# The last 256 KB of w_down as sixteen transfers of 1 to 15 and 8 rows, and final casts that wait for the matmuls alone

## The chip, the cores and the metric

The kernel runs on one core of a Trainium2 chip. Five engines execute their own instruction streams: TensorE (matmuls), VectorE, ScalarE, GpSimd and SyncE (SP), which here only issues DMA transfers. Data moves from HBM into SBUF through the core's 16 DMA engines. Engines and transfers are ordered by semaphores: an instruction waits until a semaphore has a value, and adds to one when it is done. The metric is the time of one execution in microseconds of device time; 180.47 us is the median of three runs before the change (179.78 to 180.82).

## What is computed

The reference is two layers of attention and a gated feed-forward block, run twice with the same weights, for four decode tokens:

```python
x = x + attn(layernorm(x), k_cache, v_cache, wq, wo)   # 32 heads, 8 kv heads, last 2048 of 8192 positions
x = x + glu(layernorm(x), w_gate, w_up, w_down)        # h = sigmoid(x @ w_gate) * (x @ w_up);  h @ w_down
x = x + attn(layernorm(x), k_cache, v_cache, wq, wo)
x = x + glu(layernorm(x), w_gate, w_up, w_down)
```

x is 4 x 512 (bf16), the feed-forward width is 1792, so w_down is 1792 x 512, 1.8 MB. Almost all bytes are the K and V windows (16.8 MB each for the 4 sequences) and the weights, which are read again in the second round as far as they were not kept.

## The kernel before

The kernel is written as a plan. `P.op(engine, name, duration, emit, r, w, banks)` records an operation with what it reads and writes as tokens, and `_Plan.op` turns these into dependencies: a reader depends on the last writer of a token, a writer on the readers since then or, without readers, on the last writer (lines 57 to 69), and users of one PSUM bank from different engines depend on each other. `_schedule` then orders each engine's operations by an estimate of their times; SP's transfers keep the order in which they were recorded. `_assign_sync` gives every operation a semaphore: each compute engine has one of its own, and SP's transfers take 24 in turn, each transfer also depending on the one that used its semaphore before. It then keeps the waits that are not already implied.

SBUF holds an arena of 50 slots of 4 KB per partition. `load` (line 496) records a transfer into a pair of slots with `dma` (line 395), which is one `dma_start` on SP. Transfers are recorded as soon as slots come free, so SP's queue runs far ahead of their use: the second w_gate and w_up, then w_down, wait in the queue while attention is still being computed.

w_down is laid out so that partition p holds rows 14p to 14p+13; a piece (a, b) takes b-a of these 14 rows of each partition. In the second round `bounds_of(1)` makes three pieces: rows 0 to 7 (1 MB), 8 to 11 (512 KB), 12 and 13 (256 KB, one contiguous 2 KB row for each of 128 partitions). They are the last three transfers before the output.

At the very end `glu(1, ..., last=True)` computes the gate and up projections, transposes them on VectorE, forms h in `hT` (line 1348), and multiplies with w_down piece by piece (`e_d`, line 1356): for each of the 14 rows four matmuls, one for each 128 output columns, so 32, 16 and 8 matmuls for the three pieces, all adding into one PSUM bank in which the residual x already lies (line 1306). Each piece's matmuls wait for that piece's transfer. Then four casts (line 1373) move 128 columns each to `orow`, a view of `ebuf`: ScalarE takes groups 0 and 2, VectorE 1 and 3. Each names as written, besides its own token `("oc", g)`, the token `("e", g // 2)` of its half of `ebuf`; groups 0 and 1 so share one, and 2 and 3. Last, SP issues the output transfer, which waits for the casts.

Of the kernel before, what the change touches and what calls it, by code (L numbers as in the profile page):

```python
# [254 lines left out]
class _SlotPool:  # L255
# [16 lines left out]
    bw_8k=421.0, bw_4k=409.0, bw_3k=405.0, bw_1k=347.0,  # L272
# [6 lines left out]
def build(nc, A_x, A_k, A_v, A_wq, A_wo, B_wg, B_wu, B_wd, out, cfg=None):  # L279
# [11 lines left out]
    NB, SQ, D = A_x.shape  # L291
# [7 lines left out]
    NFC = F // 128  # L299
# [16 lines left out]
    wd_d = B_wd.rearrange("(p k) n -> p k n", p=128)  # L316
# [5 lines left out]
    with es:  # L322
        def sb(name, shape, dt):
            return es.enter_context(nc.sbuf_tensor(name, shape, dt))
# [35 lines left out]
        hT = sb("hT", [128, NFC * NB], BF16)  # L360
# [13 lines left out]
        PBS = (2, 3)  # L374
# [8 lines left out]
        def tile_ap(s):  # L383
            return arena[:, s * SLOT:(s + 2) * SLOT]

        def tok(s):
            return [("slot", s), ("slot", s + 1)]

        def c_dve(n, rate=None):
            return tm["dve_fix"] + n * (tm["dve_f32"] if rate is None else rate)  # L390
# [4 lines left out]
        def dma(name, dst, src, w, r=(), rate="bw_4k", nbytes=None, sem=None):  # L395
            if nbytes is None:
                nbytes = dst.partition_size() * dst.free_nbytes()
            o = P.op("sync", name, 0.0, lambda e, dst=dst, src=src: e.dma_start(dst, src),  # L398
                     r=r, w=w, dma_bytes=nbytes, dma_rate=tm[rate])
            if sem is not None:  # L400
                o.sem = sem
                o.inc = 16
            return o


        loads = []
        where = {}
        left = {}
# [51 lines left out]
        def need(name):  # L460
            while name not in where:
                take_load()
            return where[name]

        def done(name):
            left[name] -= 1
            if left[name] == 0:
                s = where.pop(name)
                if name in on_free:
                    on_free[name](s)  # L470
                else:
                    pool.release(s)
                fill()
# [13 lines left out]
        def load_half(name, src, rate, size, where_):  # L487
            left[name] = 1
            homes[name] = [where_]
            on_free[name] = lambda s: hfree.add(s)  # L490

            def emit(s):
                dma(str(name), slot_ap(s)[:, 0:size], src, w=[("slot", s)], rate=rate)
            loads.append((name, emit))

        def load(name, n_use, rate, part):
            left[name] = n_use

            def emit(s):
                src = part[1]  # L500
                dst = tile_ap(s)[:, 0:part[0]]
                if name[0] in ("wg", "wu"):
                    dst = tile_ap(s).rearrange("p (f n) -> p f n", f=2)[:, :, 0:F]
                elif len(src.shape) == 3 and not part[2]:
                    dst = dst.rearrange("p (f n) -> p f n", f=src.shape[1])
                dma(str(name), dst, src, w=tok(s), rate=rate)
            loads.append((name, emit))
# [8 lines left out]
        def bounds_of(k):  # L516

            return [(a, min(NFC, a + 4)) for a in range(0, NFC, 4)] if k < NG else bounds[:-1] + [(bounds[-1][0], NFC - 2), (NFC - 2, NFC)]
# [31 lines left out]
        def load_glu(k):  # L550
            for nm, src in (("wg", wg_d), ("wu", wu_d)):
                if k == 0:
                    for c in range(NC):
                        load_half((nm, c, k), src[:, c, :], "bw_3k", F,
                                  (((GB, 0), (GB, 1), (GA, 0), (Y, 0)), ((Y, 1), (Z, 0), (GB, 0), (GB, 1)))[nm == "wu"][c])
                    continue
                for cc in range(NC // 2):
                    load((nm, cc, k), 2, "bw_3k", (2 * F, src[:, 2 * cc:2 * cc + 2, :], False))
            for (a, b) in bounds_of(k):
                if k == 0:  # L560
                    load_half(("wd", a, k), wd_d[:, a:b, :].rearrange("p k n -> p (k n)"), "bw_4k", (b - a) * D,
                              ((GA, 0), (Y, 0), (Y, 1), (Z, 0))[a // 4])
                else:
                    load(("wd", a, k), 1, "bw_8k", ((b - a) * D, wd_d[:, a:b, :], False))


        STASH = SB + PBS
# [48 lines left out]
        def keep_half(s):  # L616
# [9 lines left out]
             r=[("ones_f",)], w=[("e", 0)])  # L626
# [6 lines left out]
        for jh in range(2):  # L633
            for bp in range(2):
                for i in range(2):
# [7 lines left out]
                         r=[("ones_f",), ("perm",)], w=[("perm", jh, bp, i)])  # L643
# [5 lines left out]
             r=[("ones_f",)], w=[("msk_s",)])  # L649
        P.op("vector", "msk_s2", 100.0, lambda v: v.tensor_scalar(msk_s[:, :], msk_s[:, :], -1.0e30, None, ALU.mult),  # L650
             r=[("msk_s",)], w=[("msk_s",)])
        P.op("gpsimd", "msk_m", 200.0,
             lambda g: g.affine_select(msk_m[:, :], ones_f[:, 0:2], [[-1, 2]], ALU.is_equal, 0.0, base=0, channel_multiplier=1),
             r=[("ones_f",)], w=[("msk_m",)])
        P.op("vector", "sel_f", 200.0,
             lambda v: v.tensor_reduce(sel_f[:, :], perm[:, :].rearrange("p (g x) -> p x g", x=NR), AXX, ALU.add),
             r=perms, w=[("sel_f",)])
        P.op("gpsimd", "sel_b", 200.0, lambda g: g.tensor_copy(sel_b[:, :], sel_f[:, :]),
             r=[("sel_f",)], w=[("sel_b",)])
        P.op("vector", "sel_r", 100.0,  # L660
             lambda v: v.tensor_reduce(sel_r[:, :], sel_f[:, :].rearrange("p (g y) -> p y g", g=2), AXX, ALU.add),
             r=[("sel_f",)], w=[("sel_r",)])
        P.op("vector", "eyew", 200.0,
             lambda v: v.tensor_reduce(eyew[:, 96:128], ident.rearrange("p (a j) -> p j a", a=4), AXX, ALU.max),
             r=[("e", 0), ("eyew0",)], w=[("eyew",)])
        P.op("vector", "maskp", 200.0,
             lambda v: v.tensor_reduce(maskp[:, :], ident.rearrange("p (a j) -> p a j", a=4), AXX, ALU.max),
             r=[("e", 0)], w=[("maskp",)])
        P.op("vector", "maskb", 100.0,
             lambda v: v.tensor_reduce(maskb[:, :], maskp[:, :].rearrange("p (j b) -> p b j", j=2), AXX, ALU.max),  # L670
             r=[("maskp",)], w=[("maskb",)])
# [3 lines left out]
             r=[("eyew",)], w=[("maske",)])  # L675
        P.op("vector", "mod4", 100.0,
             lambda v: v.tensor_reduce(mod4[:, :], ey.rearrange("p (e m) -> p m e", m=REP), AXX, ALU.max),
             r=[("eyew",)], w=[("mod4",)])
# [4 lines left out]
             r=[("mod4",), ("maskp",)], w=[("selm",)])  # L683
# [4 lines left out]
             r=[("e", 0)], w=[("permo",)])  # L688
# [4 lines left out]
             r=[("sel_r",)], w=[("maskr",)])  # L693

        o = P.op("scalar", "x_in", 1300.0, lambda e: e.dma_start(x_nat, x_d), w=[("prow",)])
# [585 lines left out]
        def glu(k, b0, b1, last=False):  # L1281
# [31 lines left out]
            for n, nm in enumerate(("wg", "wu")):  # L1313
                for c in range(NC):
                    name = (nm, c if k == 0 else c // 2, k)
                    s = need(name) + (0 if k == 0 else c % 2)

                    def e_g(pe, c=c, s=s, n=n):
                        last = None
                        for g in range(4):  # L1320
# [4 lines left out]
                         r=[("slot", s), ("xn",)], w=[("gu", n)], banks=(gub[n],))  # L1325
                    done(name)
                if n == 0:
                    variance()
                P.op("vector", "gt%s%d" % (nm, k), c_dve(NF),
                     lambda v, n=n: v.transpose(ebuf[:, 0:NF],  # L1330
                                                ps[:, gub[n], 0:NF].rearrange("p (x k) -> p k x", k=NFC)),
                     r=[("gu", n)], w=[("e", 0), ("e", 1)], banks=(gub[n],))

                if n == 0:
                    P.op("vector", "gs%d" % k, c_dve(NH),
                         lambda v: v.tensor_tensor(egv, tv, lnr[:, 0:nb].unsqueeze(1).broadcast_to([128, NFC, nb]), ALU.mult),
                         r=[("e", 0), ("e", 1), ("lnr", 0)], w=[("eg",), ("q", 0)])
                    P.op("scalar", "gex%d" % k, c_act(NH),
                         lambda a: a.activation(eg[:, 0:NH], eg[:, 0:NH], ACTF.Exp, scale=-1.0),
                         r=[("eg",)], w=[("eg",)])  # L1340
# [3 lines left out]
                         r=[("eg",), ("lnd",)], w=[("eg",)])  # L1344
# [4 lines left out]
                 r=[("e", 0), ("e", 1), ("eg",), ("q", 0)], w=[("hT",)])  # L1349
            if last:  # L1350
                x_rows()
                for (a, b) in bounds_of(k):
                    name = ("wd", a, k)
                    s = need(name)

                    def e_d(pe, a=a, b=b, s=s):
                        last_ = None
                        src = tile_ap(s)
                        for fc in range(a, b):
                            for g in range(NC):  # L1360
                                o = (fc - a) * D + g * 128
                                last_ = pe.matmul(ps[32 * g:32 * g + NB, PBS[0], 0:128], hT[:, fc * NB:(fc + 1) * NB],
                                                  src[:, o:o + 128], start=False, stop=(fc == NFC - 1),
                                                  skip_group_check=True)
                        return last_
                    P.op("tensor", "gd%d_%d" % (k, a), (b - a) * 200.0, e_d,
                         r=tok(s) + [("hT",)], w=[("orow",)], banks=(PBS[0],))
                    done(name)
                orow = ebuf[0:NB, 0:half].bitcast(BF16)
                for g in range(NC):  # L1370
                    eng, f = ("scalar", "copy") if g % 2 == 0 else ("vector", "tensor_copy")
                    P.op(eng, "oc%d" % g, c_dve(128),
                         lambda e, g=g, f=f: getattr(e, f)(orow[:, g * 128:(g + 1) * 128], ps[32 * g:32 * g + NB, PBS[0], 0:128]),
                         r=[("orow",)], w=[("oc", g), ("e", g // 2)], banks=() if g else (PBS[0],))
                dma("out", out_d, orow, w=[("out_dram",)], r=[("oc", g) for g in range(NC)], rate="bw_1k", nbytes=NB * D * 2,
                    sem=("out",))
                return
            for (a, b) in bounds_of(k):
                name = ("wd", a, k)
                s = need(name)  # L1380

                def e_d(pe, a=a, b=b, s=s):
                    last = None
                    src = slot_ap(s)
                    for fc in range(a, b):
# [7 lines left out]
                     r=tok(s)[:1] + [("hT",)], w=[("cb",)], banks=(CB,))  # L1393
# [6 lines left out]
                 r=[("cb",)] + xts, w=xts, banks=(CB,))  # L1400
# [16 lines left out]
        load_wo(HKV // 2 - 1)  # L1417
        loads.append((GB, lambda s: None))
        load_glu(0)
        load_wq(1)  # L1420
        v_tiles = {}
# [21 lines left out]
        attn_second()  # L1443
        attn_add(2)
        glu(1, 0, NB, True)
        assert not loads

# [67 lines left out]
```

## Time and profile before

One execution was profiled:

| | |
|---|---|
| time of the profiled execution | 179.53 us |
| its span, first to last instruction | 177.7 us |
| median of three runs | 180.47 us (179.78 to 180.82) |
| granted TensorE clock, mean | 0.923 (0.50 after 160 us) |
| bytes read from HBM | 70.26 MB, 395 GB/s over the span |
| last three w_down transfers issued (SP) | 152.91, 157.23 and 158.57 us |
| output issued / landed | 176.04 / 177.27 us |

The page gives each engine's busy time and its share of the span, then the span in 40 slices whose digits are busy tenths. The chain of waits follows the last instruction back through what released it. A timeline line has start, duration, engine, line, operation, what it writes and reads, and in brackets how long the engine was idle before and what ended that. PEld is TensorE loading the small operand of a matmul. SPq and the like are an engine's sequencer, which waits, branches and issues. A landing is the moment at which a DMA engine's share of a transfer adds to the transfer's semaphore; a transfer is complete when all have.

### The profile page before, as it was taken

What the parts mean: (1) busy time and instruction counts of PE and PEld (TensorE: products, weight loads), DVE (VectorE), ACT (ScalarE), POOL (GpSimd) and SP (SyncE); (2) the same over time, 40 slices, a digit from 0 to 9 for tenths busy, and PEclk for the clock granted to TensorE, in tenths of its full rate; (3) what the DMA queues carried; (4) which work ended last, traced back from release to release, by engine and by line L of the source; (5) the groups of instructions that cost most, each with busy time, mean ns of one, the idle gap of its engine ahead of it and who ended that gap; (6) DMA issues with size and microseconds to landing.
All of it is one profiled execution on the core that took longest, in us unless ns stands there. A gap on an engine that the chain in (4) does not pass through costs nothing.

```text
span 177.7 us, 3886 instructions
## 1 busy us (share of the span) xinstructions
PE 102.3 (58%) x1641; PEld 55.0 (31%) x1653; DVE 104.7 (59%) x256; ACT 32.7 (18%) x87; POOL 21.6 (12%) x88
## 2 busy tenths in 40 slices
PE   0635326472933626506427847455967999876663
PEld 0202111242521512403415842141323444345321
DVE  7308997848476384593573573332299999752351
ACT  2002031221030300301102001000143454440011
POOL 6100010101010100100101000000011443342000
PEclk9999999999999999999999999999988888885555
DMA  5999999999999999999999999999999999999990
GB/s 193 426 426 424 422 422 413 420 420 419 419 417 422 415 422 422 413 417 424 420 419 422 405 406 368 411 395 408 410 382 365 428 424 422 411 421 403 408 367 23
DMA packets 12738, 70.52 MB, mean 397 GB/s; under 512 B 1320, under 2 KB 1328, under 8 KB 6576
## 3 DMA queue, kind: packets, MB, share of 16 engines
q1 hardware_dynamic: 12712, 70.26, 97.1%
q8 instruction: 13, 0.21, 0.5%
q14 instruction: 5, 0.04, 0.1%
q10 hardware_dynamic: 8, 0.00, 0.0%
HBM read 70.26 MB, written 0.00 MB: 395 GB/s over the span
## 4 chain that ended last, share of the span: by engine, by line
DMA 35%; DVE 32%; PE 21%; SPq 3%; issue 3%; ACT 3%; POOL 0%; DVEq 0%; ACTq 0%
DMA arena<-in_A_v_cache_dram 15%; DMA arena<-in_B_w_down_dram 13%; DVE arena L841 11%; PE ps L870 7%; PE ps L960 5%; DVE nmax L883 5%; DMA arena<-in_A_wq_dram 4%; DMA arena<-in_B_w_gate_dram 4%; SPq L398 3%; PE ps L859 2%; DVE arena L1051 2%; DVE ebuf L918 2%; DVE nmax L887 2%; DVE mxt L891 2%; PE ps L1147 2%
## 5 line engine op out<-in xcount | busy, mean ns | idle before, releaser
L841 DVE STREAM_TRANSPOSE arena<-arena 128x1024 f32<-128x1024 f32 x32 | 37.0, 1203 | 0.0
L870 PE MATMUL ps<-arena,qbd 128*32 128x512 bf16 x256 | 25.6, 536 | 0.1
L883 DVE TENSOR_REDUCE nmax<-ps 128x1 f32<-128x512 f32 x16 | 10.9, 682 | 19.3 <-PE ps L870 19.2
L960 PE MATMUL ps<-ebuf,arena 128*128 128x8 bf16 x576 | 17.6, 168 | 7.3 <-DMA arena<-in_A_v_cache_dram 4.1
L859 PE MATMUL ps<-msk_m,msk_s 128*32 128x512 bf16 x64 | 8.4, 518 | 23.0 <-DVE arena L841 21.8
L960 PEld LDWEIGHTS ps<-ebuf,arena 128*128 128x128 bf16 x576 | 16.7, 104 | 9.2 <-DMA arena<-in_A_v_cache_dram 5.1
L898 ACT ACTIVATE prow<-ps,nmax 128x512 bf16<-128x512 f32 x16 | 11.0, 687 | 34.1 <-DVE nmax L895 29.5
L834 ACT CAST qbd<-ps 128x256 bf16<-128x256 f32 x16 | 5.9, 370 | 44.9 <-PE ps L870 35.0
L927 POOL CAST s<-psm 128x1 bf16<-128x1 f32 x9 | 1.7, 188 | 83.6 <-ACT prow L898 83.6
L870 PEld LDWEIGHTS ps<-arena,qbd 128*32 128x32 bf16 x256 | 8.4, 121 | 10.3 <-issue 7.2
L782 PE MATMUL ps<-arena,xn 128*4 128x512 bf16 x64 | 8.4, 579 | 5.4 <-DMA arena<-in_A_wq_dram 5.1
L913 ACT CAST prow<-ps 128x512 bf16<-128x512 f32 x16 | 9.4, 586 | 11.4 <-PE ps L1042 3.0
L1321 PE MATMUL ps<-arena,xn 128*4 128x448 bf16 x64 | 7.5, 552 | 3.1 <-DMA arena<-in_B_w_up_dram 1.9
L918 DVE STREAM_TRANSPOSE ebuf<-prow 128x256 f32<-128x256 f32 x16 | 7.0, 435 | 3.9 <-ACT prow L913 3.7
L859 PEld LDWEIGHTS ps<-msk_m,msk_s 128*32 128x32 bf16 x64 | 1.7, 98 | 24.1 <-DVE arena L841 22.6
L794 DVE STREAM_TRANSPOSE ebuf<-ps 128x512 f32<-128x512 f32 x3 | 2.1, 716 | 10.6 <-PE ps L782 10.5
L760 ACT ACTIVATE lnv<-ps 128x4 f32<-128x4 f32 x4 | 0.7, 174 | 41.4 <-PE ps L756 41.4
L1042 PE MATMUL ps<-arena,ebuf 128*32 128x512 bf16 x112 | 8.2, 417 | 0.1
L829 PE MATMUL ps<-qh,eyew 32*128 32x64 bf16 x64 | 5.6, 217 | 4.2 <-ACT qbd L834 2.4
L968 DVE TENSOR_TENSOR onb<-ps,rinv 128x16 bf16<-128x16 f32 x9 | 1.6, 183 | 9.5 <-PE ps L960 9.5
L1147 PE MATMUL ps<-onp,arena 128*128 128x16 bf16 x144 | 5.3, 175 | 2.4 <-DVE onp L983 2.1
L1330 DVE STREAM_TRANSPOSE ebuf<-ps 128x448 f32<-128x448 f32 x4 | 2.6, 650 | 5.8 <-PE ps L1321 5.8
(111 smaller groups left out, 132.7 us busy)
## 6 DMA issues: line engine op xcount, KB each, us to landing
arena<-in_A_v_cache_dram SPq DMA_DIRECT2D x27, 1024.0 KB, 22.4
arena<-in_A_k_cache_dram SPq DMA_DIRECT2D x16, 1024.0 KB, 25.1
arena<-in_A_wq_dram SPq DMA_DIRECT2D x4, 1024.0 KB, 7.8
arena<-in_A_wq_dram SPq DMA_DIRECT2D x8, 512.0 KB, 6.5
arena<-in_A_wo_dram SPq DMA_DIRECT2D x3, 1024.0 KB, 26.2
arena<-in_B_w_down_dram SPq DMA_DIRECT2D x4, 512.0 KB, 6.4
arena<-in_B_w_gate_dram SPq DMA_DIRECT2D x4, 448.0 KB, 8.6
arena<-in_B_w_up_dram SPq DMA_DIRECT2D x4, 448.0 KB, 5.0
```

Source lines behind the costliest of these rows:

```text
L782: last = pe.matmul(ps[32 * hh:32 * hh + NB, qb, :], xn[:, c * NB:(c + 1) * NB], src[:, o + hh * 512:o + (hh + 1) * 512], start=(c == 0), s ...
L841: P.op("vector", "T%d_%d" % (h, t), c_dve(1024), lambda v, v32=v32: v.transpose(v32, v32), r=[("slot", 4 * h + t)], w=[("slot", 4 * h + t)])
L859: last = pe.matmul(ps[32 * gi:32 * gi + 32, bank, :], msk_s[:, :], msk_m[:, :].unsqueeze(1).broadcast_to([128, 256, 2]), start=True, stop= ...
L870: last = pe.matmul(ps[32 * gi:32 * gi + 32, bank, :], qbd[:, q0:q0 + 32], kt[:, cp // 2, cp % 2, jh * NJ:(jh + 1) * NJ, :], start=False, s ...
L883: lambda v: v.tensor_reduce(nmax[:, k2:k2 + 1], ps[:, bank, :], AXX, ALU.max),
L898: lambda a: a.activation(prow[:, :].rearrange("p (m x t) -> p m x t", x=32, t=2), ps[:, bank, :].rearrange("p (m t x) -> p m x t", x=32, t ...
L913: P.op("scalar", "pc" + tag, c_act(512), lambda a: a.copy(prow[:, :], ps[:, pb, :]), r=[("ppb", pb)], w=[("prow",)], banks=(pb,))
L918: P.op("vector", "pt" + tag, c_dve(256), lambda v: v.transpose(et, prow[:, :].bitcast(F32)), r=[("prow",)], w=[("e", k2)])
L960: last = pe.matmul(ps[:, ob, bp * 8:bp * 8 + 8], src[:, j * 128:(j + 1) * 128], ev[:, j % 2, j % 16 // 2, x0:x0 + 8], start=(j == 0), stop ...
L1042: last = pe.matmul(ps[32 * g:32 * g + 32, ob, :], ew[:, g, mq, t], src.rearrange("p (m t d) -> p t m d", t=2, d=128)[:, t], start=(n == 0) ...
L1147: last = pe.matmul(ps[:, WB, c * NR:(c + 1) * NR], tile_ap(s)[:, o + r_ * D + c * 128:o + r_ * D + (c + 1) * 128], ov[:, r_ * NR:(r_ + 1) ...
L1321: last = pe.matmul(ps[32 * g:32 * g + NB, gub[n], 0:NF], xn[:, c * NB:(c + 1) * NB], slot_ap(s)[:, g * NF:(g + 1) * NF], start=(c == 0), s ...
```

## The change

The 256 KB piece is no longer one transfer of 128 partitions but sixteen, of 1, 2, 3 and so on to 15 partitions, and a last one of 8 (together 128). Each has its own semaphore and its own token `("part", i)`; the eight matmuls of the piece read all sixteen tokens. The parts take over the dependencies of the first one, which waits for the slots. Since semaphores are given in turn, six of the parts wait for the transfers that used theirs before. The other edit takes `("e", g // 2)` out of what the four final casts write, so that each depends on the matmuls alone.

```diff
+                elif b < NFC:
+                    load(("wd", a, k), 1, "bw_8k", ((b - a) * D, wd_d[:, a:b, :], False))
                 else:
-                    load(("wd", a, k), 1, "bw_8k", ((b - a) * D, wd_d[:, a:b, :], False))
+                    load_last(("wd", a, k), a, b)
+
+        PARTS = list(range(1, 16)) + [8]
+        def load_last(name, a, b):
+            left[name] = 1
+            def emit(s):
+                dst = tile_ap(s)[:, 0:(b - a) * D].rearrange("p (f n) -> p f n", f=b - a)
+                p0, first = 0, None
+                for i, n in enumerate(PARTS):
+                    o = dma("%s_%d" % (name, i), dst[p0:p0 + n], wd_d[p0:p0 + n, a:b, :],
+                            w=[("part", i)] + (tok(s) if i == 0 else []), rate="bw_4k")
+                    if first is not None:
+                        o.deps.update(first.deps)
+                    first = first or o
+                    p0 += n
+            loads.append((name, emit))
...
                     P.op("tensor", "gd%d_%d" % (k, a), (b - a) * 200.0, e_d,
-                         r=tok(s) + [("hT",)], w=[("orow",)], banks=(PBS[0],))
+                         r=tok(s) + [("hT",)] + ([("part", i) for i in range(len(PARTS))] if b == NFC else []),
+                         w=[("orow",)], banks=(PBS[0],))
...
-                         r=[("orow",)], w=[("oc", g), ("e", g // 2)], banks=() if g else (PBS[0],))
+                         r=[("orow",)], w=[("oc", g)], banks=() if g else (PBS[0],))
```

More of the change, by code (lines that the diff above doesn't have):

```diff
@@ L562, in load_glu @@
                               ((GA, 0), (Y, 0), (Y, 1), (Z, 0))[a // 4])
-                else:
-                    load(("wd", a, k), 1, "bw_8k", ((b - a) * D, wd_d[:, a:b, :], False))
+                elif b < NFC:
+                    load(("wd", a, k), 1, "bw_8k", ((b - a) * D, wd_d[:, a:b, :], False))
+                else:
+                    load_last(("wd", a, k), a, b)
[12 more added lines that the diff above has]
+                    p0 += n
+                assert p0 == 128
+            loads.append((name, emit))
         STASH = SB + PBS
```

## The prediction

> **What bounds the kernel now.** I read the page's share of busy time and its slices first, then the chain that ended last in order of time, then the timeline of the last microseconds, then those microseconds cut into windows.
>
> ```profile
> span 177.7 us, 3886 instructions
> PE 102.3 (58%) x1641; PEld 55.0 (31%) x1653; DVE 104.7 (59%) x256; ACT 32.7 (18%) x87; POOL 21.6 (12%) x88
> DMA  5999999999999999999999999999999999999990
> q1 hardware_dynamic: 12712, 70.26, 97.1%
> ```
>
> No engine is busy for more than 59%, while the transfers are above 90% in 38 of 40 slices: the kernel reads 70 MB without a pause, and nothing in this change alters that. What is left is the tail behind the last byte. The chain, start and length in us:
>
> ```profile
> 157.23 16.74 DMA arena<-in_B_w_down_dram
> 173.97 0.04 issue
> 174.01 0.60 PE ps L1362 x16
> 174.61 0.03 issue
> 174.64 0.41 PE ps L1362 x8
> 175.05 0.02 issue
> 175.07 0.27 ACT ebuf L1373
> 175.34 0.02 issue
> 175.36 0.28 DVE ebuf L1373
> ```
>
> The chain does not run through the transfer that is changed. Its DMA piece ends at 173.97, which is the landing of the 512 KB piece before it; 16 matmuls of that piece follow, and only then the 8 of the 256 KB piece. The timeline of the same stretch:
>
> ```profile
> 174.01 0.31 PEld L1362 LDWEIGHTS ps<-arena,hT 128*4 128x4 bf16 x16 [0.50 <-DMA arena<-in_B_w_down_dram]
> 174.64 0.10 PEld L1362 LDWEIGHTS ps<-arena,hT 128*4 128x4 bf16 x8 [0.32 <-DMA arena<-in_B_w_down_dram]
> 175.07 0.54 ACT L1373 CAST ebuf<-ps 4x128 bf16<-4x128 f32 x2 [5.00 <-PE ps L1362]
> 175.36 0.61 DVE L1373 CAST ebuf<-ps 4x128 bf16<-4x128 f32 x2 [3.20 <-ACT ebuf L1373]
> 176.04 0.34 SPq L398 DMA_DIRECT2D out_dram<-ebuf  x1
> ```
>
> VectorE sits idle until ScalarE's first cast is over, though both read the same finished sums. The windows show how the DMA engines run out one after the other (columns: busy us of each engine, clock, DMA share, GB/s):
>
> ```profile
> 171.00:172.00 1.00, 0.63 (x12) 0.13 (x4) 0.70 (x2) 0.00 (x0) 0.00 (x0) 0.50 1.00 404
> 172.00:173.00 1.00, 0.22 (x12) 0.23 (x16) 0.16 (x1) 0.00 (x0) 0.00 (x0) 0.50 0.70 274
> 173.00:174.00 1.00, 0.80 (x32) 0.51 (x20) 0.00 (x0) 0.00 (x0) 0.00 (x0) 0.50 0.39 135
> ```
>
> The trace's semaphore records give the landings engine by engine. The 512 KB piece lands on the first of 16 engines at 171.94 and on the last at 173.97; the 256 KB piece between 172.61 and 174.60. So each engine needs 0.63 to 0.67 us for its eight 2 KB rows (packets start 80 ns apart), and the engines stand 2.0 us apart before they begin. The lags behind the first are 0.08, 0.26, 0.32, 0.45, 0.56, 0.59, 0.71, 0.92, 0.99, 1.29, 1.72, 1.73, 1.74, 1.80 and 2.03 us. Instruction fetches of 16 KB, 0.93 to 1.12 us each on one engine, are what I take to have made most of it.
>
> **The change part by part.** The profiled execution took 179.53 us with a span of 177.7. It lies 0.94 below the median of 180.47 and below all three runs shown; the sum is made on it and carried over as a difference.
>
> *Casts.* Before: ScalarE's first cast 175.07 to 175.33, VectorE's two 175.36 to 175.65 and 175.68 to 175.97, ScalarE's second done at 175.61. After the change VectorE waits for the matmuls only, so its first starts beside ScalarE's at 175.07 and its second ends at 175.07+0.28+0.02+0.29 = 175.67. The output's issue follows 0.07 later, as now. Gain 0.30. ScalarE's second cast already overlapped VectorE's first without stretching either (258 against 255 ns, 282 against 293), so the bounds are narrow, 0.27 to 0.30. Nothing else is queued behind these casts.
>
> *Waits of TensorE.* The last eight matmuls now wait for sixteen semaphores. In the built program that is eight instructions that only wait, then the ninth wait on the first weight load. The trace has no such row of waits; single ones last 51 ns on TensorE, and the next weight load starts 75 ns after such a wait starts (110.07 to 110.15, 39.89 to 39.96). Eight cost 0.41 to 0.60. They begin when the sequencer has sent off the 16 matmuls before them. It runs ahead: the instruction behind the last eight matmuls is recorded at 174.66, 0.02 after the first of them starts. So the waits begin between 174.03 and 174.19 and the last matmuls between 174.44 and 174.79, against 174.64 now. The array itself, taking four matmuls each 0.107, would be free at 174.40. I take 174.10+0.60 = 174.70, the only measured distance to a next instruction: a loss of 0.06, bounds -0.24 and +0.15. If no wait cost anything, the matmuls of the 512 KB piece would still hide the transfer until 174.40.
>
> *Sixteen issues on SP.* Before, the changed transfer is issued at 158.57 and takes 2.12 because the queue is full. An issue that does not block costs 0.33 to 0.61, the output's four rows 0.34; sixteen take 5.3 to 9.8 us. Six of them also wait for semaphores last used by six value loads, landed between 143.6 and 156.3, before the issue. A full queue held 80 to 107 descriptors an engine, and the fullest engine gets 32 for this transfer instead of 9; 23 more drain at 0.14 each in 3.2 us. All are out by 158.6+9.8+3.2 = 171.6 at worst, the earliest engine turns to them at about 171.5, and SP has nothing else before the output at 176.04. Cost 0; the cover is those 13 us of queued weights.
>
> *The landing of the 256 KB.* The input and the output, four rows each, show four data packets and four semaphore packets, while 128 rows make sixteen semaphore packets. So a part of n rows occupies n engines. If each part begins with the same engine, the loads are 16, 15, 14 down to 9, then 7 down to 0 rows, in place of 8 each. A row costs 0.080 and its part's semaphore 0.006. Bounds: with the many rows on the engines that are early, the last landing is 174.00; with them on the late ones, 173.97+16x0.086 = 175.34; shuffled at random, half the orders lie under 175.00 and one in fifteen under 174.66. Everything up to 174.66 is hidden behind the waits. No row names the engines, so this is the open term: 0 to +0.7. I take 0, since lags grow in an orderly ramp of 2.0 us and the new loads are a ramp of 1.3 us: they either fit together or oppose.
>
> [...]
>
> Sum: -0.30 +0.06 +0 +0 = -0.24: 179.29 in a profiled execution, 180.2 for the median.
>
> **Rivals.** *The ramp opposes the lags.* The last landing is 174.9 to 175.34, the matmuls start 0.04 to 0.1 later instead of at 174.64: +0.3 to +0.8, with the casts 0.0 to +0.5, so 180.5 to 181.0. For it: random orders mostly do this. Against: nothing but the ramp's shape.
>
> *Slower: the small transfers queue by number.* The kernel never had more than 11 transfers in flight; with the parts it would have 23. If the queue holds at most 12, the last five parts go out only after 174.0, when the 512 KB has landed, at 0.34 each; the output needs 1.23 from issue to landing, so the last part lands near 177.0, +2.4-0.3: 182.6. With 16 only the last part waits, for 173.97: 175.3, +0.65-0.3, about 180.8. It decides from a limit of 14 down. Against: issue blocked at 7, 8, 9 and 10 transfers, always near the same number of descriptors.
>
> *The transfer is hidden and the waits too.* The matmuls start at 174.40: -0.24-0.30, so 179.9. For it: the sequencer's lead; against: 75 ns a wait.
>
> **How the numbers follow.** Forecast 0.47 (own range 179.9 to 180.4, which includes the third rival), opposing ramp 0.35, limit by number 0.13, and 0.05 for other executions in which the engines stand further apart than in this profile and the ramp recovers up to 1 us. About 0.5%, 0.9 us, is what a measurement tells from no change. Faster by more needs 179.57, which the terms reach only with that last case or by the spread of the runs (179.78 to 180.82): 0.11. Slower by more needs 181.37: the limit by number, and the worst third of the opposing ramp with the port rule's bound: 0.24. Within: 0.65. The range 179.5 to 181.7 leaves out the stronger half of the limit by number.
>
> **What would show it.** VectorE's first cast starting with ScalarE's; eight waits on TensorE between the last two groups of matmuls and their spacing; sixteen issues on SP ended before 171; the last part's landing against 174.6. The prediction is wrong if the last matmuls wait for a landing after 174.7, or if an issue on SP begins after 172.

## The result and the profile after

The changed kernel took 182.01 us in the median of 15 runs, the kernel before 180.82 us beside it: 1.0077 times as long, with a 95% interval of 1.0055 to 1.0099. A second set of runs gave 1.0093 (1.0058 to 1.0127). So it is slower, by 1.4 us in the first set and 1.7 us in the second, where 180.2 us and no measurable change had been forecast.

The profiled execution after took 182.01 us with a span of 180.2 us. The page's first line and its transfers:

```profile
span 180.2 us, 3909 instructions
DMA  4999999999999999999999999999999999999960
q1 hardware_dynamic: 12824, 70.26, 96.1%
```

As before, the transfers are busy to the end and as many bytes move. The end of the chain, start and length in us:

```profile
158.42 18.01 DMA arena<-in_B_w_down_dram
176.42 0.04 issue
176.47 0.59 PE ps L1382 x8
177.06 0.37 issue
177.43 0.41 PE ps L1382 x8
177.84 0.02 issue
177.87 0.28 DVE ebuf L1394
178.15 0.32 DVEq L1495
```

Two things are new: the 0.37 us between the two groups of matmuls, and one cast in place of two. The timeline shows the casts side by side:

```profile
177.40 0.13 PEld L1382 LDWEIGHTS ps<-arena,hT 128*4 128x4 bf16 x8 [0.62 <-issue]
177.87 0.60 DVE L1394 CAST ebuf<-ps 4x128 bf16<-4x128 f32 x2 [3.97 <-PE ps L1382]
177.87 0.54 ACT L1394 CAST ebuf<-ps 4x128 bf16<-4x128 f32 x2 [7.77 <-PE ps L1382]
178.55 0.27 SPq L398 DMA_DIRECT2D out_dram<-ebuf  x1
```

The windows of the same stretch (columns: busy us of each engine, clock, DMA share, GB/s):

```profile
171.00:172.00 1.00, 0.00 (x0) 0.00 (x0) 0.00 (x0) 0.00 (x0) 0.00 (x0) 0.50 0.99 404
172.00:173.00 1.00, 0.98 (x16) 0.38 (x16) 0.01 (x1) 0.00 (x0) 0.00 (x0) 0.50 0.93 330
173.00:174.00 1.00, 0.37 (x8) 0.00 (x0) 0.86 (x2) 0.00 (x0) 0.00 (x0) 0.50 0.64 178
174.00:175.00 1.00, 0.06 (x6) 0.07 (x8) 0.00 (x0) 0.00 (x0) 0.00 (x0) 0.50 0.41 139
```

Compare bytes with busy share. Before, 274 GB/s went with a share of 0.70, which is 391 GB/s for a full share. Here 178 GB/s go with 0.64, which is 278. The engines are busy and move less. The trace's packet records say how: a packet of 8 KB takes 314 ns before, and 401 to 448 ns between 172.6 and 173.7 here; one of 4 KB 223 ns on average in the half microsecond from 173.0 against 159; one of 2 KB 117 against 84. The packets of 8 KB and 4 KB belong to transfers that the change does not touch.

The spans differ by 2.5 us, but not all of that is the change. I followed the last of 16 engines from piece to piece in the landings:

| | before | after | difference |
|---|---|---|---|
| last landing of w_up | 170.25 | 171.98 | +1.73 |
| from there to that of the 1 MB piece | 2.48 | 2.91 | +0.43 |
| to that of the 512 KB piece | 1.24 | 1.53 | +0.29 |
| to that of the 256 KB | 0.63 | 0.47 | -0.16 |
| to the last eight matmuls | 0.04 | 0.54 | +0.50 |
| casts | 0.97 | 0.68 | -0.29 |

The first packet of a part moves at 172.26, so the 1.73 us were there before any of them. Of the 1.73, 0.82 us is there already on the first of the 16 engines (168.15 before, 168.97 after), and 0.91 is a wider spread of the engines (2.10 and 3.01 us). Both differ between executions: in a second profile of the changed kernel, shown below, w_up lands at 170.97 with a spread of 2.07. The execution profiled before was an early one (179.53 against a median of 180.82 in these runs). The rest of the 2.5 us, +0.77, lies behind w_up.

### The profile page after: what moved, and what is told of

It is laid out like the page before. It is cut to its first block, busy times and chain, and to the rows that moved or that the text cites. A ratio compares the mean times of both kernels' runs of the same rounds, so it can differ in the third digit from the quotient of the medians.

```text
span 180.2 us, 3909 instructions
## 1 busy us (share of the span) xinstructions
PE 101.9 (57%) x1641; PEld 54.9 (30%) x1653; DVE 103.9 (58%) x256; ACT 32.7 (18%) x87; POOL 21.6 (12%) x88
## 4 chain that ended last, share of the span: by engine, by line
DVE 35%; DMA 33%; PE 20%; issue 4%; SPq 3%; ACT 3%; POOL 1%; DVEq 0%; ACTq 0%
DMA arena<-in_A_v_cache_dram 15%; DMA arena<-in_B_w_down_dram 14%; DVE arena L861 11%; PE ps L890 7%; DVE nmax L903 5%; DMA arena<-in_A_wq_dram 4%; SPq L398 3%; PE ps L980 3%; PE ps L879 2%; DVE nmax L907 2%; DVE arena L1071 2%; DVE mxt L911 2%; DVE ebuf L938 2%; PE ps L1167 2%; ACT prow L918 2%
## 5 line engine op out<-in xcount | busy, mean ns | idle before, releaser
L1062 PE MATMUL ps<-arena,ebuf 128*32 128x512 bf16 x112 | 7.6, 392 | 0.2 <-DVE nmax L915 0.2
```

The lines of the kernel that those rows point to most:

```text
L1062: last = pe.matmul(ps[32 * g:32 * g + 32, ob, :], ew[:, g, mq, t], src.rearrange("p (m t d) -> p t m d", t=2, d=128)[:, t], start=(n == 0) ...
```

## The experiments

### The terms by themselves

Casts alone, on the kernel before:

```diff
-                         r=[("orow",)], w=[("oc", g), ("e", g // 2)], banks=() if g else (PBS[0],))
+                         r=[("orow",)], w=[("oc", g)], banks=() if g else (PBS[0],))
```

> The kernel before with the edit to the four casts alone; the 256 KB of w_down stays one transfer of 128 rows. Every theory has the casts as a term of its own, -0.30 us (0.27 to 0.30): VectorE's and ScalarE's first casts start together right behind the last matmul, and the output is issued 0.30 earlier. If the change's loss were hidden in the casts (two engines reading one PSUM bank at once, say), this kernel would gain less than 0.2, and the stretch would be seen in the durations of the four casts.

Measured: 0.9974 of before (0.9943 to 1.0005).

```profile
175.83 0.10 PEld L1362 LDWEIGHTS ps<-arena,hT 128*4 128x4 bf16 x8 [0.33 <-DMA arena<-in_B_w_down_dram]
176.27 0.54 ACT L1373 CAST ebuf<-ps 4x128 bf16<-4x128 f32 x2 [5.59 <-PE ps L1362]
176.27 0.60 DVE L1373 CAST ebuf<-ps 4x128 bf16<-4x128 f32 x2 [2.94 <-PE ps L1362]
176.95 0.34 SPq L398 DMA_DIRECT2D out_dram<-ebuf  x1
```

From the first cast to the output's issue 0.68 us, before 0.97 (175.07 to 176.04): 0.29 gained. The casts are not stretched by two engines reading one bank: 0.54 and 0.60 us for two of them, before 0.54 and 0.61. Since this is also the version that should beat both kernels, it ran again:

> The kernel before with the edit to the casts alone, again, as the version that should be faster than both: 0.30 faster than before, ratio about 0.998.

Measured: 0.9968 (0.9941 to 0.9995). The half of the change that pays is the edit of one token.

The change without this edit, so with sixteen parts and the casts' old tokens (the diff is against the changed kernel):

```diff
-                         r=[("orow",)], w=[("oc", g)], banks=() if g else (PBS[0],))
+                         r=[("orow",)], w=[("oc", g), ("e", g // 2)], banks=() if g else (PBS[0],))
```

> The change without its edit to the casts: sixteen transfers, sixteen semaphores, casts in a row as before. If the terms add up, it is 0.30 slower than the changed kernel, so 1.5 us slower than before (ratio 1.0077 of the changed kernel, plus 0.30). Theory (the parts slow down the other engines' packets): the 2 KB, 4 KB and 8 KB packets between 172 and 174 us are stretched against the 84, 159 and 314 ns of before, to about 117, 223 and up to 440 ns, and the 512 KB piece lands some 0.7 later behind the 1 MB piece than in the kernel before. Rival (the ramp of loads stands against the lags): packets keep their durations and only the parts land late, behind the 512 KB piece by more than 0.7. Rival (transfers queue by number): a part's issue on SP lies after 172.

Measured: 1.0134 (1.009 to 1.0178), 2.4 us slower than before. The 1.5 us above is a slip: the 1.0077 is 1.4 us, and with the 0.30 the sum asked for 1.7, which the interval allows. All sixteen issues were over at 166.7 us on SP, so the limit by number falls. Packets are stretched, if less at the peak: half-microsecond means reach 400 ns (8 KB), 228 (4 KB) and 116 (2 KB). The 1 MB piece's last landing is 2.82 us behind w_up's, the 512 KB another 1.58 (0.3 more than before, where 0.7 had been expected), the last part another 1.04. So the stretch of that theory is there, and so is a part that lands late, which only the opposing ramp had. In its chain the matmuls start on the landing, with no gap for waits:

```profile
166.36 11.77 DMA arena<-in_B_w_down_dram
178.13 0.06 issue
178.18 0.41 PE ps L1382 x8
```

The waits alone, on the kernel before:

```diff
+                if o.name == "gd1_12":
+                    for i in range(24):
+                        if ("dma", i) not in dict(o.waits) and len(old) < 15:
+                            old.append(i)
+                            eng.wait_ge(dma_sems[i], 16)
                 for (s, v) in o.waits:
                     eng.wait_ge(sem_h(s), v)
```

> The kernel before, with fifteen further waits ahead of the last eight matmuls, all for semaphores that have long reached their value: the cost of the waits by themselves. Transfers and casts are those of before. By the prediction's 75 ns for each of the waiting instructions from 174.10 on it costs 0.06 (-0.24 to +0.15 were the bounds). By the 106 ns between the changed kernel's waits, from the sequencer's end of the 512 KB piece on, it costs 0.2 to 0.4. The landings and the durations of the packets should be those of before; if they are not, waits on TensorE reach the transfers in a way that no theory here has.

The chain of its profile:

```profile
173.54 0.04 issue
173.58 0.60 PE ps L1362 x16
174.18 0.38 issue
174.56 0.41 PE ps L1362 x7
```

The groups of matmuls start 0.98 us apart where it was 0.63: the waits cost 0.35 us, as in the changed kernel (0.96 apart). From one wait to the next it is 106 ns (111 and 153 in two of the seven steps), and all lie behind the start of the 16 matmuls. The time was 1.0027 of before (0.9993 to 1.0062), which holds 0.35 us and also none; the 0.35 is the trace's. Packets and landings are those of before.

### One semaphore for the parts

```diff
+        if p is not None and o.sem != ("parts",):
...
+                    o = dma(..., rate="bw_4k", sem=("parts",))
```

All sixteen parts now add to one semaphore. The waits of TensorE shrink to one, and transfers on this semaphore do not wait for each other.

> The changed kernel, with one semaphore for all sixteen parts, so TensorE waits once, for 256, in place of eight instructions that wait for two semaphores each; transfers and casts are those of the changed kernel. If the row of waits costs what the changed kernel's trace shows (from the last landing at 176.89 to the first of the last eight matmuls at 177.43), it gains 0.34 to 0.5 against the changed kernel, and stays 0.9 to 1.1 slower than before because the landings are late all the same. If the waits were the whole loss, it would be as fast as before or 0.3 faster. If the waits only fill time in which the parts are still landing, it is the changed kernel's time.

Measured: 1.0052 (1.0017 to 1.0087). The last part landed 1.66 us behind the 512 KB piece, and the matmuls started 0.04 later. I repeated it beside the changed kernel:

> The changed kernel itself, beside the version with one semaphore on the same chip: about 1.4 us (0.8%) slower than before. By the completion theory its last landing lies 0.5 to 1.7 us behind that of the 512 KB piece, and the row of waits shows only where that is under 0.95.

> The changed kernel with one semaphore for all parts, again. If the row of eight waits is mostly hidden behind late landings, it is 0 to 0.3 us faster than the changed kernel beside it; if the waits cost what the changed kernel's one trace shows, 0.3 to 0.5.

Measured: 1.0093 (1.0058 to 1.0127) for the changed kernel and 1.0065 (1.0029 to 1.0102) with one semaphore. The two pairs differ by 0.25 and 0.28%, some 0.5 us, but the intervals overlap, so what the waits cost in the median isn't settled between 0 and 0.5. The second profile of the changed kernel shows why it varies:

```profile
164.98 12.19 DMA arena<-in_B_w_down_dram
177.17 0.05 issue
177.22 0.41 PE ps L1382 x8
```

Here the last part landed at 177.17, 2.04 us behind the 512 KB piece, and the waits were all hidden; in the first profile it landed 0.47 behind it, and the row of waits ended 0.48 us after the landing. Whichever of the two ends last sets the start of the matmuls; in the four traces in which sixteen parts have sixteen semaphores (one of them follows below) the landings did in three.

Where do landings come from? The last packet of a part in this execution was written at 175.30, its landing is 177.17: 1.87 us. In the kernels whose 256 KB are one transfer the same distance is 0.41 to 0.47, but for one of 0.57 (the 512 KB piece as eight transfers of neighbouring rows, below). In the five traces with the ramp of side-by-side parts it is 0.81 to 1.93. On one engine the additions mostly follow each other 0.15 to 0.22 us apart, though a row and its semaphore packet take 0.09. In the changed kernel's first profile an engine still adds 0.155 us apart at 176.58 to 176.89, when no packet of a transfer is on its way any more. So the additions of an engine behave as a queue of their own, slower than its rows.

The semaphore's packets of these transfers are short, 9 ns for most; the landings say that with one row each the additions come at one in 0.15 us or slower. What takes this time, no run here shows.

### Where the rows lie

The changed kernel with the rows of each part 8 partitions apart:

```diff
+                    c = min(n, 16 - n) - 1
+                    rows = slice(c + 8 * n_in[c], c + 8 * (n_in[c] + n - 1) + 1, 8)
+                    n_in[c] += n
+                    o = dma(..., dst[rows], wd_d[rows, a:b, :], ...)
```

> The changed kernel with the same sixteen transfers of 1 to 15 and 8 rows, sixteen semaphores and new casts, but the rows of each transfer lie 8 partitions apart in place of side by side. Neighbour theory (many engines writing to neighbouring partitions at once slow down every packet): no stretch any more, so 8 KB packets 314 ns, 4 KB 160, 2 KB 84 between 172 and 175 us; w_up to the 1 MB piece 2.48 on the last engine and 1 MB to 512 KB 1.25, where the kernels with parts had 2.83 to 2.91 and 1.53 to 1.58; 0.3 to 0.7 us faster than the changed kernel. Completion theory (an engine needs 0.155 to 0.2 us from one part's semaphore addition to the next, however soon the row is written): the additions of one engine stay at least 0.155 apart, the last part lands later than 0.63 behind the 512 KB, and the kernel stays slower than before by 0.3 or more. If the stretch comes from the number of small packets and not from where they go, durations and time are those of the changed kernel.

Measured: 1.0101 (1.0056 to 1.0147). The packets were stretched as much, 8 KB to 401 ns on average in the half microsecond from 172.5 and to 439 at most, and the last part landed 1.34 us behind the 512 KB piece. An issue took 0.34 to 0.80 us on SP, where it was 0.24 to 0.38 side by side, but the last was over at 172.08, before the first part moved at 172.26. As I had put it, the stretch spoke against neighbours.

Eight equal transfers of 16 rows, one semaphore, casts as before, the rows side by side or 8 partitions apart:

```diff
-        PARTS = list(range(1, 16)) + [8]
+        PARTS = [16] * 8
...
+                    o = dma(..., dst[p0:p0 + n], wd_d[p0:p0 + n, a:b, :], ...)     # side by side
+                    o = dma(..., dst[i:128:8], wd_d[i:128:8, a:b, :], ...)         # 8 apart
```

> Casts as before. The last 256 KB as eight transfers of 16 neighbouring rows, one semaphore and one wait: every engine gets eight rows, as before, but one at a time, so no ramp of loads and no row of waits. Completion theory: eight additions on each engine 0.155 to 0.2 apart, so 1.25 to 1.6 us from the 512 KB piece to the last part in place of 0.63: slower than before by 0.6 to 1.0. Neighbour theory on top: packets stretched by 1.3 to 1.4 as in the changed kernel, 0.3 to 0.7 more. Rival (the uneven loads were the loss): no slower than before by more than 0.1.

> As the kernel with eight transfers of 16 rows, with the 16 rows of a transfer 8 partitions apart. Completion theory: the same 1.25 to 1.4 us from the 512 KB piece to the last part, slower than before by 0.6 to 0.8. Neighbour theory: no packet stretched, so 0.3 to 0.7 faster than with neighbouring rows. Rival (the uneven loads were the loss): the time of before.

Measured: 1.0067 (1.0031 to 1.0103) and 1.0085 (1.005 to 1.0121). The last part landed 1.45 and 1.38 us behind the 512 KB piece, as the additions ask; both stretch packets (8 KB to at most 366 and 504 ns). Even loads lose as much as the ramp with one semaphore and the same casts would (1.2 and 1.5 us here; 0.9 and 1.2 there, and 0.3 for the casts), so the uneven loads are not needed for the loss.

Four transfers of 32 rows, 4 partitions apart:

```diff
+        PARTS = [32] * 4
...
+                    o = dma(..., dst[i:128:4], wd_d[i:128:4, a:b, :], ...)
```

> Casts as before. Four transfers of 32 rows, the rows 4 partitions apart, one semaphore: two rows an engine and transfer, four additions an engine. If an addition is a limit of one in 0.155 to 0.17 us, two rows of 84 ns cover it, the last part lands 0.65 to 0.75 behind the 512 KB piece and the time is that of before within 0.1. If each addition costs 0.09 us on top of the rows, it lands 0.3 later than that and the kernel is 0.3 slower than before.

Measured: 1.0012 (0.9979 to 1.0046). No packet is stretched, the last part lands 0.64 us behind the 512 KB piece and 0.42 behind its last packet. Two rows an engine cover the additions. The windows around the first packets of the parts, at 173.15 (columns as above):

```profile
172.00:173.00 1.00, 0.49 (x8) 0.24 (x12) 0.00 (x0) 0.00 (x0) 0.00 (x0) 0.50 0.97 397
173.00:174.00 1.00, 0.85 (x16) 0.14 (x4) 0.52 (x1) 0.00 (x0) 0.00 (x0) 0.50 0.98 391
```

This left three suspects for the stretch: a single row per engine, the rate of additions, or the places after all. To tell them apart, first the piece of 512 KB, then that of 1 MB comes as eight transfers of 16 neighbouring rows, with the rest as before:

```diff
+        PARTS = [16] * 8
...
-                elif b < NFC:
+                elif b != 12:                                                  # 8 for the 1 MB piece
                     load(("wd", a, k), 1, "bw_8k", ((b - a) * D, wd_d[:, a:b, :], False))
```

> Casts as before, and the last 256 KB are one transfer again. It is the 512 KB piece before it that comes as eight transfers of 16 neighbouring rows, of 4 KB each: eight additions an engine, one row for each, as in the kernel with eight transfers of 2 KB rows, but a row takes 159 ns. Rate theory (an engine can add once in 0.155 to 0.17 us): the rows are nearly slow enough, packets keep 314, 160 and 84 ns, the 512 KB lands 1.25 to 1.4 behind the 1 MB piece and the kernel is within 0.2 us of before. Count theory (each transfer of one row costs about 0.09 more, whatever its size): 0.6 to 0.8 later and packets stretched, about the time of the kernel with eight transfers of 2 KB rows.

> Casts as before. The 1 MB piece comes as eight transfers of 16 neighbouring rows of 8 KB, the 512 KB and the 256 KB as one transfer each. An engine adds once in 0.32 us, half of the rate at which additions pile up. If the stretch comes with transfers that give an engine a single row, whatever the rate, it is as in the kernel with eight transfers of 4 KB rows or worse: 8 KB packets above 450 ns, 1.5 us slower than before or more. If it comes with the rate of additions, packets keep 314, 160 and 84 ns and the time is that of before within 0.3.

Measured: 1.0100 (1.0067 to 1.0133) and 1.0329 (1.0272 to 1.0386). In the second most 8 KB rows take 0.5 us or longer, so an engine adds no more often than that, and the stretch is the worst of all. So the rate of additions falls as the cause of the stretch. Windows of the second:

```profile
168.00:169.00 1.00, 1.00 (x13) 0.25 (x6) 0.09 (x1) 0.00 (x0) 0.00 (x0) 0.50 1.22 315
169.00:170.00 1.00, 0.40 (x6) 0.32 (x10) 0.70 (x2) 0.47 (x3) 0.00 (x0) 0.50 1.04 198
170.00:171.00 1.00, 0.89 (x8) 0.08 (x8) 0.65 (x3) 0.25 (x1) 0.00 (x0) 0.50 1.14 195
```

All engines are busy and move 195 GB/s, where 410 to 420 was usual. Then two rows an engine again, but 32 neighbours, `PARTS = [32] * 4` with `dst[p0:p0 + n]`:

> Casts as before. The last 256 KB as four transfers of 32 neighbouring rows, two rows an engine. The kernel with 32 rows 4 partitions apart stretched no packet. If the stretch comes with transfers that give an engine a single row, there is none here either: 314, 160 and 84 ns, the last part 0.65 to 0.75 behind the 512 KB piece, the time of before within 0.3. If it comes with where the rows lie, and rows 4 apart were the one good spacing, packets are stretched by 1.2 or more, and it is 0.4 or more slower than before.

Measured: 1.0059 (1.0023 to 1.0094). In the microsecond from 172 the 8 KB packets take 478 to 502 ns, in the next two 426 and 667, and the 1 MB piece lands 3.56 us behind w_up, where it was 2.48 before:

```profile
171.00:172.00 1.00, 0.45 (x8) 0.22 (x12) 0.00 (x0) 0.00 (x0) 0.00 (x0) 0.50 1.05 406
172.00:173.00 1.00, 0.89 (x16) 0.15 (x8) 0.48 (x1) 0.00 (x0) 0.00 (x0) 0.50 0.91 223
```

The transfers number and weigh the same as in the kernel with 32 rows 4 apart; only the places differ. 223 GB/s (busy share 0.91) stand against 391 (0.98). So the single row is not needed for the stretch and the places matter, but not as near and far. From the 1 MB piece on the landings are almost those of before: 1.22 us to the 512 KB piece and another 0.70 to the last part, against 1.24 and 0.63. So the stretch alone cost 1.1 us here, and four additions of two rows an engine cost next to nothing, where eight of one row took 1.38 and 1.45. The last pair takes the 1 MB and the 512 KB piece again, with `dst[i:128:8]`:

> As the kernel with the 1 MB piece in eight transfers of 16 neighbouring rows of 8 KB, with the 16 rows 8 partitions apart. If the place of the rows is what stretches packets, it is near the time of before (within 0.5 us) and 8 KB packets take 314 to 330 ns. If a single row per engine and transfer is enough, wherever it lies, packets take 500 ns and more and it is 3 us or more slower than before, as with neighbouring rows (ratio 1.033).

> As the kernel with the 512 KB piece in eight transfers of 16 neighbouring rows of 4 KB, with the rows 8 partitions apart. By the place of the rows: no stretch from the rows themselves, the time of before within 0.5, unless additions at one in 0.165 us pile up too, which would show as landings that fall behind the packets by more than the usual 0.45 us. By the single row: the 1.8 us of the neighbouring rows (ratio 1.010).

Measured: 1.0172 (1.0141 to 1.0204) and 1.0126 (1.0086 to 1.0166). Windows of the first:

```profile
167.00:168.00 1.00, 1.00 (x12) 0.14 (x4) 0.00 (x0) 0.00 (x0) 0.00 (x0) 0.50 1.06 417
168.00:169.00 1.00, 1.00 (x14) 0.61 (x10) 0.65 (x1) 0.32 (x3) 0.00 (x0) 0.50 1.12 267
169.00:170.00 1.00, 0.46 (x8) 0.00 (x0) 0.56 (x3) 0.40 (x3) 0.00 (x0) 0.50 1.06 218
```

From 417 to 218 GB/s, a factor of 0.52, with most 8 KB packets between 540 and 640 ns. Both of my alternatives for these runs had taken 8 apart for a harmless place, so they tell the single row from the places only if it is one, and these runs do not tell the two apart.

By the place of the rows, the runs show:

| rows of a transfer | 8 KB packets, ns | GB/s (busy share 0.91 or more) |
|---|---|---|
| 128 (before) | up to 325 | 397 to 404 |
| 32, 4 apart | up to 324 | 391 to 397 |
| 32 neighbours | 426 to 502, one 667 | 223 |
| 16, 8 apart, 8 KB rows | mostly 540 to 640 | 218 |
| 16 neighbours, 8 KB rows | mostly 530 to 800 | 195 to 198 |

The stretch appears for the last three placements and for neither of the first two, and it takes about half of the rate (195 to 223 GB/s). The other kernels with slices of 2 KB and 4 KB rows were slower than before as well; three of them show the stretch in numbers: 8 KB packets to at most 366 ns (2 KB rows, 16 neighbours) and 504 ns (8 apart), and 217 GB/s at a busy share of 1.01 (4 KB rows, 16 neighbours). With 2 KB rows 16 neighbours did not stretch more than 16 rows 8 apart (4 KB packets to 246 ns on average in the worst half microsecond of either). I changed placement only in spacing and number; what it is about a place that stretches packets, no run shows. A rival stays untested: each part reads the rows of `wd_d` that it writes, so the places in HBM changed together with the partitions, and no run moves one without the other. Nor did any run give an engine a single row in a transfer whose place left packets at 325 ns or less, so how much of the slow additions comes with the places is open. What no run explains is why packets of 8 KB whose engines write elsewhere are slowed as evenly as the rest.

## Why the prediction was wrong, step by step

- *What bounds the kernel.* Right. The end is a chain of landings, matmuls, casts and output before and after.
- *Casts, -0.30.* Right: 0.29 and 0.29 in two traces, within the bounds of 0.27 to 0.30, and alone 0.9974 and 0.9968.
- *Waits of TensorE, +0.06.* Mis-sized: 0.35 by themselves, above the bound of +0.15. The 75 ns from one wait to the next instruction were read off single waits; in a row, and with two semaphores each, they are 106 ns apart. They began about where I had put them, 0.11 us after the first of the 16 matmuls where I took 0.09. The third rival, in which no wait costs anything, falls with this.
- *Sixteen issues on SP, 0.* Right. The last was over at 165.37, before any part moved. The slower rival, a limit by number, falls. (It also used 1.23 us from the output's issue to its landing; the last of the four landings is at 177.31 and not at 177.27, so 1.27. Nothing else rests on that.)
- *The landing of the 256 KB, 0 with bounds 0 to +0.7.* This is the step that failed, at two terms. "A row costs 0.080 and its part's semaphore 0.006" took the semaphore's packet for its landing. The landings of one engine are 0.15 to 0.22 us apart, so sixteen parts need 2.4 us and more on an engine that I gave 1.38. And the step priced only the parts. It left the transfers beside them at full speed, while the 512 KB piece landed 0.4 to 0.7 us later behind w_up, and the 1 MB piece 0.1 to 0.4. The rival of the opposing ramp had the right place, a last part that lands late, but a different reason, and its 180.5 to 181.0 was too little as well.
- *The port rule's bound*, which the forecast's chance of a slower result names: no run shows this term, and what the runs showed in its place is a stretch that goes with the place of the rows, 401 to 448 ns for 8 KB packets beside the sixteen parts against 314 before. The sum had no loss for neighbouring rows. The trace of before has one transfer of few rows into SBUF, the input's, with four packets of 1 KB that took 44 ns each, all within 99 ns. That row was too little to carry it: 1 KB on each of four engines, once.
- *The ramp.* It neither fitted nor opposed for good; that changed with the execution. In the first profile of the changed kernel 11 of the 128 additions came after the last landing of the 512 KB piece, in the second 61, and the last part landed 0.47 and 2.04 us behind it. So the 0.47 of the first profile was luck. On average the ramp made no difference: eight even transfers, without ramp, took as long from the 512 KB piece to the end (1.38 and 1.45 us) as the ramp (0.47, 2.04, 1.04, 1.66 and 1.65, mean 1.37).

The sum with measured terms: in five traces without stretch (before, casts alone twice, waits alone, 32 rows 4 apart) the last landing lies 4.35 to 4.38 us behind w_up's. In the five with the ramp side by side (the changed kernel twice, old casts, one semaphore twice) it lies 4.91, 6.20, 5.44, 6.08 and 5.85 behind it, 5.70 on average: +1.33. Of this 0.6 lies between w_up and the 512 KB piece (4.32 against 3.73), the stretch, and 0.74 behind it, the additions with what stretch is left. With -0.29 for the casts that is +1.04, and the waits add 0 to 0.5. Measured are 1.4 (1.0 to 1.8) and 1.7 (1.0 to 2.3) us. The range to 181.7 missed 182.01 because its worst landing was 0.7 us late, where 0.55 to 1.84 were measured.

## What to carry to other kernels

When a transfer is cut up, look at which partitions each slice takes. Slices of 16 or 32 neighbouring rows, and of 16 rows 8 apart, could halve the rate of everything in flight beside them (195 to 223 GB/s against 391 to 404); a cut into four interleaved slices of 32 rows cost nothing that could be measured (1.0012, 0.9979 to 1.0046). Give each engine at least as many rows per transfer as cover the 0.15 to 0.22 us from one semaphore addition to the next (two rows of 84 ns did), and read a transfer's end from the semaphore's landing, not from its last packet. When the last landings are what a tail waits for, compare landings from a common point, since w_up landed 1.73 us apart in two executions before the change could act.

## What the runs showed of the hardware that I had not expected

- Packets stretch together, in unrelated transfers too: of the data packets that began in the changed kernel between 173.0 and 173.5 us none kept its time of before (2 KB 102 to 134 ns against 84, 4 KB 193 to 246 against 159, 8 KB 440 and 448 against 314). In the kernel with 8 KB rows 8 apart most 8 KB packets between 168.7 and 173.4 us took 540 to 640 ns.
- With one row an engine and transfer, the additions of one engine were at least 0.15 us apart, and the last lagged up to 1.93 us behind the last packet, where 0.41 to 0.47 was usual.
- A TensorE instruction that waits for two semaphores is recorded with 51 ns, and in the changed kernel's row of eight the next began 105 to 111 ns after it, most of them 106. With the waits alone, where all values were long there, it was 106 ns too (once 111, once 153).
- In the changed kernel each part of k rows shows k landings and, 0.4 to 0.6 us after its issue on SP began, one more addition. The kernel waits for 16 a transfer, so that one must count 16 - k: the part of one row counted 15 at 160.21 and its row landed at 173.21.
